# The last store of a fused attention and mixture kernel: four transfers cut by 32 partitions instead of by column block, a copy between the matmuls, another buffer for one scaled copy

## The chip, the core and the metric

The kernel runs on one core of one Trainium2 chip. A core has a matrix engine (TensorE; in the profile PE for its matmuls and PEld for its weight loads), a vector engine (VectorE, DVE), a scalar engine (ScalarE, ACT), a general engine (GpSimd, POOL) and a sync engine (SP) that only issues transfers; ACT and POOL issue transfers too. Transfers run on 16 DMA engines. Matmul results go to PSUM, whose banks hold 512 float32 per partition; everything else is in SBUF, 128 partitions wide.

The metric is device time in microseconds, the median of several executions. One execution was also profiled; its rows give a start and a duration for each instruction, counted from the start of its span.

## The reference, cut to what matters

```python
# attention: batch 4, heads 4, seq 1088, head_dim 32, r = 8
a = einsum('rd,bhsd->bhsr', S1, x);  b = einsum('rd,bhsd->bhsr', S2, x)
phi(x) = outer product of a and b, 64 features per row
kv = phi(k)^T v;  z = sum over s of phi(k)
attn = (phi(q) kv) / (phi(q) z + 1e-6)
x = attn, heads joined: 4352 rows of 128

# mixture: E = 4 experts, F = 1024 hidden
p = domain_probs / (sum(domain_probs) + 1e-9)
out = sum over e of p[:, e] * (relu(x @ w1[e]) @ w2[e])        # 4352 x 128, float32
```

## The kernel before, in words

The 4352 tokens are worked in ten chunks of 128, 448, seven times 480, and 416 columns. Tokens lie along the free dimension and the 128 features on the partitions; token t of a batch sits at row 34·(t mod 32) + t div 32 of that batch in DRAM, so that a block of 32 tokens has its rows 34 apart. For each chunk and each of the four experts the kernel makes eight blocks of 128 hidden rows (`first`: three matmuls a block, L1141, L1142, L1193) and multiplies them by the second weight matrix (`passed`: L1274). Matmuls of higher precision are made of several passes on split operands ("a", "b", "d"), which is why one expert has two PSUM accumulators, `o0` and `o1`. Which product is issued at which step is a list written by hand (`DEAL`, `DEAL_END` and others, worked off by `behind`); the schedule is manual, so each engine runs its instructions in the order in which the code emits them. The framework adds the semaphores, from the tiles that the instructions read and write.

When an expert is done, its `o0` is copied out by ACT with a scale of 1 + R12 (L1277) into the tile `ev`, `o1` is added, and the sum is multiplied by the gate and added to `total`. For most experts this is `close` and `gather`, partly on POOL (L1361, L1368, L1370). Where `gather` takes `o1` through ACT, the copy lies in a tile `rest` (L1358). Both `ev` and `rest` have one buffer.

The last expert of the last chunk (`at_end`: 416 tokens) goes another way, since nothing follows that could hide its end. `finish` does the three steps on DVE in two column halves, 256 and 160 (L1285, L1286, L1287), and leaves the sum with features on the partitions in `last_sum`. Two of the eight hidden blocks are multiplied with the tokens on the output's partitions (`by_token`, L1301): four column blocks `c` of 128, 128, 128 and 32 tokens in one PSUM bank `y`. Behind the second of them, four products of `last_sum` with an identity matrix (L1308, two matmuls each) turn the sum around and add it into the same bank. Then the bank is copied to `rows` in SBUF: ACT takes the first two column blocks (L1313), DVE the third and the fourth (L1314, L1315; the fourth has 32 partitions). Four transfers, one for each column block, send `rows` to `out` (L1318): SP block 0, ACT block 2, SP block 1, ACT block 3. In DRAM the access pattern of a transfer of 128 tokens begins with a dimension of 4, then 32 rows that lie 34 rows apart, then 128 contiguous floats; in SBUF it has 128 partitions of 128 floats.

The framework's closing instructions carry line L1534: SP waits there for every transfer, and then the engines meet.

Of the kernel before, what the change touches and what calls it, by code (L numbers as in the profile page):

```python
# [9 lines left out]
F32 = mybir.dt.float32  # L10
# [8 lines left out]
def _ap(t, p0: int, np_: int, off: int, free):  # L19

    p = list(t.ap)[0]
    return bass.AP(t.tensor, t.offset + p0 * p[0] + off, [[p[0], np_]] + [list(d) for d in free])
# [3 lines left out]
def kernel(  # L26
# [24 lines left out]
    nc = tc.nc  # L51

    P = 128
    HP = 64
    B, H, S, D = q.shape
    E, DM, F = w1.shape
    R = 8
    R2 = 2 * R
    G = S // 32
# [6 lines left out]
    CW = 480  # L66
# [48 lines left out]
    mpool = ctx.enter_context(tc.tile_pool(name="moe", bufs=2))  # L115
# [5 lines left out]
    def psum(pool, tag):  # L121
        return pool.tile([P, 512], F32, tag=tag, name=tag)
# [72 lines left out]
    def last_of(m, e, o):  # L195
        deal = deal_of(m, e)
        return max((p for p in deal if p[0] in ("ab" if o == 0 else "d" if at_end(m, e) else "dx")), key=lambda p: (deal[p], list(deal).index(p)))
# [4 lines left out]
    def second_weight(e, b):  # L202

        at = split_at(b)
        return w2_of[e, 0 if in_three(b) else 1][:, DM * at : DM * (at + 1)]
# [170 lines left out]
    def parts(m):  # L376

        c, end, at = START[m], START[m] + CHUNKS[m], 0
        while c < end:
            n = min(end, (c // S + 1) * S) - c  # L380
            yield c // S, c % S, n, at
            c, at = c + n, at + n
# [690 lines left out]
    def at_end(m, e):  # L1073
        return (m, e) == (NC - 1, E - 1)

    def block_of(m, e, k):
        return (THREE + tuple(OTHER))[k] if at_end(m, e) else k
# [180 lines left out]
    begun_o, evs = set(), {}  # L1258

    def passed(m, e, what, k, hd):  # L1260

        n, o = CHUNKS[m], 0 if what in "ab" else 1
        if what == "x" and at_end(m, e):
            return by_token(m, e, k, hd)
        if (m, e) not in acc:
            acc[m, e] = [None, None]
        if acc[m, e][o] is None:
            acc[m, e][o] = psum(ps_o, f"o{o}")
        first_one = (m, e, o) not in begun_o
        begun_o.add((m, e, o))  # L1270
        last = last_of(m, e, o) == what + str(k)
        b = block_of(m, e, k)
        w, h = (second_weight(e, b), hd) if what == "x" else (w2_parts[e][b]["abd".index(what)], hd["abd".index(what)])
        nc.tensor.matmul(acc[m, e][o][:, 0:n], w, h, start=first_one, stop=last)  # L1274
        if last and o == 0:
            evs[m, e] = mpool.tile([P, CW], F32, tag="ev", bufs=1, name="ev")
            nc.scalar.activation(evs[m, e][:, 0:n], acc[m, e][0][:, 0:n], ACTF.Copy, scale=1.0 + R12)  # L1277
        if last and o == 1:
            finish(m, e) if at_end(m, e) else close(m, e)

    def finish(m, e):

        n, o1, ev, g = CHUNKS[m], acc.pop((m, e))[1], evs.pop((m, e)), gate.pop((m, e))
        for x in (slice(0, 2 * P), slice(2 * P, n)):
            nc.vector.tensor_tensor(out=ev[:, x], in0=ev[:, x], in1=o1[:, x], op=ALU.add)  # L1285
            nc.vector.tensor_tensor(out=ev[:, x], in0=ev[:, x], in1=g[:, x], op=ALU.mult)  # L1286
            nc.vector.tensor_tensor(out=ev[:, x], in0=ev[:, x], in1=total[m][:, x], op=ALU.add)  # L1287
        last_sum[0] = ev
# [3 lines left out]
    def by_token(m, e, k, hd):  # L1292

        n = CHUNKS[m]
        if last_rows[0] is None:
            last_rows[0] = psum(ps_h, "h")
            last_rows.append(lpool.tile([P, 4 * P], F32, tag="kn", name="rows"))
        y, rows = last_rows
        cols = [(c, min(P, n - c)) for c in range(0, n, P)]
        for c, w in cols:  # L1300
            nc.tensor.matmul(  # L1301
                y[0:w, c : c + P], hd[:, c : c + w], second_weight(e, block_of(m, e, k)),
                start=(k == N3 and c == 0), stop=False, skip_group_check=True,
            )
        if k < FB - 1:
            return
        for c, w in cols:
            nc.tensor.matmul(  # L1308
                y[0:w, c : c + P], last_sum[0][:, c : c + w], eye[0][:, :],
                start=False, stop=True, skip_group_check=True,  # L1310
            )
        ((b, at, _, _),) = parts(m)
        nc.scalar.copy(rows[:, 0 : 2 * P], y[:, 0 : 2 * P])  # L1313
        nc.vector.tensor_copy(rows[:, 2 * P : 3 * P], y[:, 2 * P : 3 * P])  # L1314
        nc.vector.tensor_copy(rows[0 : n - 3 * P, 3 * P :], y[0 : n - 3 * P, 3 * P :])  # L1315
        for queue, c in ((nc.sync, 0), (nc.scalar, 2), (nc.sync, 1), (nc.scalar, 3)):
            c, w = cols[c]
            queue.dma_start(  # L1318
                bass.AP(out.tensor, out.offset + (b * S + (at + c) // 32) * DM, [[DM, w // 32], [G * DM, 32], [1, DM]]),
                rows[0:w, c : c + P],  # L1320
            )

    eye = [None]
# [91 lines left out]
    def close(m, e):  # L1415

        nonlocal ending
        ended = gather(m, e)
        next(ended)
        ending = chain(ending, ended)  # L1420
        closed[0] = m, e
# [5 lines left out]
    def behind(at):  # L1427

        was = closed[0]
        while due and due[0][0] <= at:  # L1430
            _, _, _, i, j, what = due.pop(0)
            m, kq = steps[i]
            e, f = divmod(kq, NP)
            if what:
                passed(m, e, what, 2 * f + j, hid[i][j])
                continue
            second(i, j)
            if i == NQ - 1:
                unit_project(0)
                unit_rows(0)  # L1440
            if f == NP - 1 and j == 1:
                close(m, e)
        return closed[0] != was
# [16 lines left out]
    for i in range(len(steps) + LA):  # L1460
# [4 lines left out]
        if i < len(steps):  # L1465
            m, kq = steps[i]
# [72 lines left out]
```

## Time and profile before

| what | value |
|---|---|
| median of 3 runs | 447.35 us (447.32 to 447.63) |
| the profiled execution: its own time | 447.11 us |
| its span, first to last instruction | 445.1 us |
| granted TensorE clock, mean | 0.997 |
| PE busy | 437.4 us, 98% |
| DVE busy | 386.5 us, 87% |
| ACT busy | 345.4 us, 78% |
| POOL busy | 166.7 us, 37% |
| last matmul of the program (L1308) ends | 438.94 us |
| last copy to `rows` (L1315) ends | 439.86 us |

A row of the timeline gives the start in the span, the duration, the engine and line, output <- inputs, the partitions and elements, and in brackets how long the engine had been idle before it and what it waited for. Rows that run together are merged ("x8"), and a merged row's second number is the stretch from its first start to its last end. "SPq" and "ACTq" are the queues of SP and ACT when they issue transfers: the duration is that of issuing, and the data moves afterwards. A table of stretches gives, for each, its length, the granted clock, the mean busy share of the 16 DMA engines and the GB/s they moved. "To landing" is the time from the start of a transfer's issue to its completion.

### The profile page before, as it was taken

Reading aid. Unit: us, or ns where it says so; the run is one execution under the profiler, and the core shown is the slowest. Engines: PE = TensorE matmul, PEld = TensorE weight load, DVE = VectorE, ACT = ScalarE, POOL = GpSimd, SP = SyncE. Lnnn points to the kernel's source line nnn. Section 1 sums busy time; section 2 is a strip of 40 time slices with the busy share of each in tenths; the row PEclk is TensorE's granted clock in tenths of the full one; section 3 lists DMA queues with packets and bytes.
Section 4 is the critical chain, followed back from the end, with each engine's and each line's share of the span. In section 5 each row is a group of like instructions: output and inputs, shape, how many; then the busy total and the mean of one; then the engine's idle time right before and its main releaser. Section 6 shows DMA issues by size and latency. Waiting matters only on the chain.

```text
span 445.1 us, 8123 instructions
## 1 busy us (share of the span) xinstructions
PE 437.4 (98%) x2770; PEld 359.6 (81%) x2770; DVE 386.5 (87%) x616; ACT 345.4 (78%) x721; POOL 166.7 (37%) x243
## 2 busy tenths in 40 slices
PE   9999999999999999999999999999999999999994
PEld 6887678888887887778887888787888888889992
DVE  5998979978999789989997898889988998899893
ACT  4478898848888688868884888687888888888881
POOL 6358523212142023213351354133335463555451
PEclk9999999999999999999999999999999999999998
DMA  7945375224602430235114511260420012002100
GB/s 224 307 114 170 86 174 112 73 56 122 149 24 45 123 90 24 74 83 143 24 28 74 143 19 41 50 159 21 71 50 21 18 46 45 23 13 43 26 20 21
DMA packets 45525, 35.02 MB, mean 79 GB/s; under 512 B 21708, under 2 KB 40268, under 8 KB 45484
## 3 DMA queue, kind: packets, MB, share of 16 engines
q1 hardware_dynamic: 43960, 33.30, 30.0%
q0 software_dynamic: 1184, 1.05, 1.0%
q8 instruction: 22, 0.36, 0.3%
q10 hardware_dynamic: 340, 0.15, 0.2%
q14 instruction: 19, 0.16, 0.1%
HBM read 29.27 MB, written 5.21 MB: 77 GB/s over the span
## 4 chain that ended last, share of the span: by engine, by line
PE 92%; DMA 3%; DVE 1%; SPq 1%; ACT 1%; issue 1%; POOL 0%; DVEq 0%; ACTq 0%
PE o L1274 40%; PE h L1141 14%; PE h L1142 14%; PE h L1193 14%; PE h L272 6%; PE o L1253 3%; DMA w_sb<-in_moe_w_dram 2%; PE h L459 1%; PE o L272 1%; DMA dp<-in_moe_domain_probs_dram 1%; PE h L1301 1%; DVE hb L1169 0%; ACT h L1143 0%; SPq L178 0%; DMA s_raw<-in_S_dram 0%
## 5 line engine op out<-in xcount | busy, mean ns | idle before, releaser
L1143 ACT ACTIVATE h<-h 128x480 f32<-128x480 f32 (+2 forms) x288 | 158.9, 552 | 63.8 <-PE h L1142 56.5
L1169 DVE SCALAR_TENSOR_TENSOR hb<-h,ha 128x480 fp32r<-128x480 f32 (+2 forms) x225 | 140.5, 639 | 28.2 <-ACT ha L1197 25.8
L1172 DVE SCALAR_TENSOR_TENSOR hd<-ha,hb 128x960 fp32r<-128x960 f32 (+4 forms) x120 | 137.9, 1149 | 11.6 <-DVE hb L1169 0.5
L1141 PE MATMUL h<-xa,wa 128*128 128x480 f32 (+2 forms) x288 | 129.5, 450 | 0.0
L1197 ACT ACTIVATE ha<-h 128x480 fp32r<-128x480 f32 (+2 forms) x225 | 126.3, 561 | 0.1
L1193 PE MATMUL h<-xd,wd 128*128 128x480 f32 (+2 forms) x288 | 108.7, 377 | 0.1
L1142 PE MATMUL h<-xb,wb 128*128 128x480 f32 (+2 forms) x288 | 108.0, 375 | 0.0
L1368 POOL TENSOR_TENSOR ev<-ev,gate 128x256 f32<-128x256 f32 (+3 forms) x52 | 46.8, 900 | 146.1 <-DVE ev L1355 138.4
L1274 PE MATMUL o<-ha,vab 128*128 128x480 f32 (+2 forms) x204 | 76.7, 377 | 0.0
L1141 PEld LDWEIGHTS h<-xa,wa 128*128 128x128 f32 x288 | 54.2, 188 | 18.0 <-issue 11.4
L1142 PEld LDWEIGHTS h<-xb,wb 128*128 128x128 f32 x288 | 54.2, 188 | 17.5 <-issue 11.7
L1274 PE MATMUL o<-hd,vd 128*128 128x480 f32 (+2 forms) x204 | 63.7, 379 | 0.2 <-DVE hd L1172 0.2
L1193 PEld LDWEIGHTS h<-xd,wd 128*128 128x128 f32 x288 | 54.0, 188 | 8.9 <-ACT h L1143 0.8
L1370 POOL TENSOR_TENSOR total<-total,ev 128x256 f32<-128x256 f32 (+3 forms) x52 | 55.7, 1072 | 4.1
L1274 PE MATMUL o<-hb,vb 128*128 128x480 f32 (+2 forms) x136 | 51.2, 376 | 0.0
L1274 PE MATMUL o<-hid,w_sb 128*128 128x480 f32 (+2 forms) x90 | 43.2, 561 | 0.0
L1274 PEld LDWEIGHTS o<-hd,vd 128*128 128x128 f32 x204 | 37.8, 188 | 6.3 <-issue 0.8
L1274 PEld LDWEIGHTS o<-ha,vab 128*128 128x128 f32 x204 | 38.3, 188 | 5.1
L1361 POOL TENSOR_TENSOR ev<-ev,rest 128x256 f32<-128x256 f32 (+2 forms) x24 | 16.9, 726 | 63.3 <-ACT rest L1358 63.3
L1207 ACT ACTIVATE hid<-h 128x480 f32<-128x480 f32 (+2 forms) x62 | 34.7, 560 | 1.5 <-PE h L1193 1.4
L1368 POOL TENSOR_TENSOR total<-ev,gate 128x256 f32<-128x256 f32 (+3 forms) x18 | 15.8, 898 | 38.4 <-issue 23.0
L1274 PEld LDWEIGHTS o<-hb,vb 128*128 128x128 f32 x136 | 25.5, 188 | 4.0 <-DVE hb L1169 0.4
(166 smaller groups left out, 466.8 us busy)
## 6 DMA issues: line engine op xcount, KB each, us to landing
gate<-gates SPq DMA_DIRECT2D x16, 240.0 KB, 3.4
kn<-in_k_dram SPq DMA_DIRECT2D x4, 544.0 KB
vn<-in_v_dram SPq DMA_DIRECT2D x16, 128.0 KB, 5.9
qp<-qd SPq DMA_DIRECT2D x8, 256.0 KB
qp<-qd SPq DMA_DIRECT2D x6, 288.0 KB, 4.7
qb<-qd SPq DMA_DIRECT2D x6, 288.0 KB
qn<-in_q_dram SPq DMA_DIRECT2D x3, 544.0 KB
w_sb<-in_moe_w_dram SPq DMA_DIRECT2D x3, 512.0 KB
```

The costliest lines, as they stand in the source:

```text
L272: nc.tensor.matmul(out(s), weights(s), moving(s), **flags)
L1141: nc.tensor.matmul(g, wa[:, e, w], xa, start=True, stop=False)
L1142: nc.tensor.matmul(g, wb[:, e, w], xb, start=False, stop=True)
L1143: nc.scalar.activation(g, g, ACTF.Copy, scale=1.0 + R12)
L1169: nc.vector.scalar_tensor_tensor(out=hb, in0=g, scalar=0.0, in1=high, op0=ALU.max, op1=ALU.subtract)
L1172: nc.vector.scalar_tensor_tensor(out=d2, in0=a2.bitcast(F32), scalar=R12, in1=b2.bitcast(F32), op0=ALU.mult, op1=ALU.subtract)
L1193: nc.tensor.matmul(g, w, x, start=False, stop=True, skip_group_check=True)
L1197: nc.scalar.activation(ha, g, ACTF.Relu, scale=NEAR)
L1207: nc.scalar.activation(hid[i][j], g, ACTF.Relu)
L1274: nc.tensor.matmul(acc[m, e][o][:, 0:n], w, h, start=first_one, stop=last)
L1368: nc.gpsimd.tensor_tensor(out=to[:, x], in0=ev[:, x], in1=g[:, x], op=ALU.mult)
L1370: nc.gpsimd.tensor_tensor(out=total[m][:, x], in0=total[m][:, x], in1=ev[:, x], op=ALU.add)
```

## The change

Three things, all at the last expert of the last chunk:

- the scaled copy of `o0` (L1277) goes to a tile with the tag `rest` instead of `ev`; `finish` works on that tile;
- in `by_token` the ACT copy of column blocks 0 and 1 is emitted behind the identity product of block 1, the DVE copy of block 2 behind that of block 2, and the DVE copy of block 3 behind that of block 3, where all copies stood behind all four products;
- the four transfers are cut by partitions: transfer `g` takes partitions 32g to 32g + 31 of all column blocks that have them (four for g = 0, three for the others). Its access pattern begins, on both sides, with a dimension of 32. SP sends g = 0 and 2, ACT sends g = 1 and 3. The 416 pieces of 512 bytes that are sent, and their places in DRAM, are the same.

```diff
         if last and o == 0:
-            evs[m, e] = mpool.tile([P, CW], F32, tag="ev", bufs=1, name="ev")
+            tag = "rest" if at_end(m, e) else "ev"
+            evs[m, e] = mpool.tile([P, CW], F32, tag=tag, bufs=1, name=tag)
             nc.scalar.activation(evs[m, e][:, 0:n], acc[m, e][0][:, 0:n], ACTF.Copy, scale=1.0 + R12)
...
         if k < FB - 1:
             return
-        for c, w in cols:
+        ((b, at, _, _),) = parts(m)
+        for i, (c, w) in enumerate(cols):
             nc.tensor.matmul(
                 y[0:w, c : c + P], last_sum[0][:, c : c + w], eye[0][:, :],
                 start=False, stop=True, skip_group_check=True,
             )
-        ((b, at, _, _),) = parts(m)
-        nc.scalar.copy(rows[:, 0 : 2 * P], y[:, 0 : 2 * P])
-        nc.vector.tensor_copy(rows[:, 2 * P : 3 * P], y[:, 2 * P : 3 * P])
-        nc.vector.tensor_copy(rows[0 : n - 3 * P, 3 * P :], y[0 : n - 3 * P, 3 * P :])
-        for queue, c in ((nc.sync, 0), (nc.scalar, 2), (nc.sync, 1), (nc.scalar, 3)):
-            c, w = cols[c]
-            queue.dma_start(
-                bass.AP(out.tensor, out.offset + (b * S + (at + c) // 32) * DM, [[DM, w // 32], [G * DM, 32], [1, DM]]),
-                rows[0:w, c : c + P],
+            if i == 1:
+                nc.scalar.copy(rows[:, 0 : 2 * P], y[:, 0 : 2 * P])
+            elif i > 1:
+                nc.vector.tensor_copy(rows[0:w, c : c + P], y[0:w, c : c + P])
+        for g in range(4):
+            t = len([w for _, w in cols if w > 32 * g])
+            (nc.scalar if g % 2 else nc.sync).dma_start(
+                bass.AP(out.tensor, out.offset + (b * S + at // 32 + g) * DM, [[G * DM, 32], [4 * DM, t], [1, DM]]),
+                _ap(rows, 32 * g, 32, 0, [[P, t], [1, DM]]),
             )
```

## The prediction, made before the result was known

> **What bounds the kernel now.** I read the page first: PE is busy 98% of the span, so up to the last matmul only PE's time counts. The change touches nothing before 434 us. What it touches lies in the last 11 us, and there PE is done at 438.94 while the span runs to 445.1: more than 6 us of copying, sending and closing. So I read the timeline of that end next.
>
> ```profile
> 434.23 0.34 PE L1274 MATMUL o<-hb,vb 128*128 128x416 f32 x1
> ...
> 434.77 0.65 PE L1274 MATMUL o<-hd,vd 128*128 128x416 f32 x2 [0.19 <-DVE hd L1172]
> ...
> 435.13 0.52 ACT L1277 ACTIVATE ev<-o 128x416 f32<-128x416 f32 x1 [0.57 <-POOL total L1370]
> ...
> 435.69 0.42 DVE L1285 TENSOR_TENSOR ev<-ev,o 128x256 f32<-128x256 f32 x1 [0.47 <-ACT ev L1277]
> ...
> 437.65 0.32 DVE L1287 TENSOR_TENSOR ev<-ev,total 128x160 f32<-128x160 f32 x1
> ...
> 437.67 1.27 PE L1308 MATMUL h<-eye,ev 128*128 128x128 f32 x8
> 438.98 0.37 ACT L1313 COPY rows<-h 128x256 f32<-128x256 f32 x1 [3.33 <-PE h L1308]
> 439.38 1.25 SPq L1318 DMA_DIRECT2D out_dram<-rows  x2
> 439.39 0.29 DVE L1314 COPY rows<-h 128x128 f32<-128x128 f32 x1 [1.42 <-ACT rows L1313]
> 439.59 0.27 DVE L1315 COPY rows<-h 32x128 f32<-32x128 f32 x1
> ```
>
> See two things. The DVE copy L1314 reads and writes other columns than the ACT copy L1313, yet it waited for it: the program orders accesses of two engines to the one PSUM bank, even two reads. That order is not one of `rows`, since SP's first transfer left at 439.38 without waiting for the DVE copies into the same tile. And the copies take 0.9 us in all (438.98 to 439.86); the other 5 us are transfers and closing. So I asked for those: the last issue on ACT's queue and its landing, and the share of the 16 DMA engines by stretch, here and where the kernel stores 128 pieces of 512 bytes elsewhere (L722).
>
> ```profile
> 440.46 0.46 ACTq L1318 DMA_DIRECT2D out_dram<-rows  x1
> ```
> ```profile
> out_dram<-rows ACTq DMA_DIRECT2D x1, 16.0 KB, 3.5
> ```
> ```profile
> 440.90:441.50 0.60, 1.00 0.28 79
> 441.50:441.90 0.40, 1.00 0.24 46
> 441.90:442.40 0.50, 1.00 0.34 88
> 442.40:442.70 0.30, 1.00 0.43 101
> 442.70:443.30 0.60, 0.51 0.30 90
> 443.30:443.50 0.20, 0.50 0.16 44
> ```
> ```profile
> 198.60:199.20 0.60, 1.00 0.72 168
> ```
>
> The last transfer, of only 16 KB, was issued at 440.46 and landed 3.5 us later, at 443.96; the rest of the span, 1.1 us, is closing. From 440.9 to 443.3 the data moved without a break, but at about 0.3 of the engines' time, some four to five of 16. At 198.6 to 199.2 stores of the same piece or a little larger kept 0.72 busy. The end is bound by transfers that use a quarter of the DMA engines.
>
> **The change part by part.**
>
> *The other buffer.* L1277 waited 0.57 us for POOL, which held `ev`. The tile `rest` was last read by POOL at 421.4 (L1361), so L1277 can start when its bank is done: 434.23 + 0.34 = 434.57, about 434.6 instead of 435.13. L1285 then waits for `o1`, whose last matmul ends at 434.77 + 0.65 = 435.42: 435.46 instead of 435.69, 0.23 us sooner. None of it counts: the first half of the sum was ready at 437.03 (L1287: 436.60 + 0.43) for a product that PE reached at 437.67, and the second half at 437.97 for block 2, which PE reached at 438.11. What covers it is PE's own row of 16 matmuls L1301 ahead. The ACT order is unchanged, and nothing else on SP or POOL is passed. Zero; without that cover the gain would be 0.23 at most.
>
> *The copies between the products.* The first two column blocks are in PSUM at 438.39 (the timeline cut at that place gives 437.89 + 0.50). If bank order holds for a matmul behind a read as it does for a read behind a read, each later step waits for the one before. Hand-overs from the rows: PE to ACT 0.04 (438.94 to 438.98), ACT to PE 0.05 (L1143 ends 428.96, the weight load of L1193 starts 429.01), DVE to PE 0.05 (L1172 ends 434.72, L1274 loads at 434.77). One block of two matmuls from a standing start takes 0.49 (437.67 to 438.16), the block of 32 takes 0.41 (438.54 to 438.94). Sum: ACT copy 438.39 + 0.04 + 0.37 = 438.80; block 2 on PE + 0.05 + 0.49 = 439.34; DVE copy + 0.04 + 0.29 = 439.67; block 3 + 0.05 + 0.41 = 440.13; DVE copy + 0.04 + 0.27 = 440.44. Before, the last copy ended at 439.86: 0.58 later. Queued behind the waits on PE is only the rest of this chain; behind those on DVE nothing; on ACT the transfers. The nearest row for PE's restart is L1301 after its wait, and it shows nothing longer. If the matmuls did not wait, the copies would end at about 439.30 (ACT 438.80, DVE + 0.03 + 0.29, and the last one 0.20 + 0.27 - 0.29 behind), 0.56 sooner.
>
> The Trainium skill, in "PSUM — Partial Sum Buffer", section "PSUM bank collisions raise a hardware error", says that no two of the three engines may touch the same bank and quadrant at once and that programs must guard PSUM by bank, not by address. By that rule the sum is the one with the waits, 440.44; without it, 439.30. The wait of 1.42 on L1314 agrees, between two reads; no row of before shows a matmul behind such a read.
>
> *The transfers.* Removed: three of 64 KB and one of 16; added: one of 64 and three of 48, the same 416 pieces. SP's pair begins when the last copy is done (g = 0 needs block 3): 440.44 + 0.03 = 440.47 instead of 439.38. ACT's pair needs blocks 0 to 2 only: 439.67 + 0.03 = 439.70, as before (439.71), its second issue 0.75 behind as before, 440.45. The second SP issue comes 0.47 behind the first by L722 (four issues in 1.85, one 0.45) or 0.67 by L1318 (439.38 to 440.05). I take 0.5, since the form of L722 is nearer. From issue to landing I have these rows, all stores out of 32 partitions, of L722 and then L1336:
>
> ```profile
> DMA to landing us min/median/max: 1.7/1.7/1.7
> ```
> ```profile
> DMA to landing us min/median/max: 1.6/1.9/2.5
> ```
>
> L722 is the same form: 32 partitions, four pieces of 512 bytes from each, to DRAM. I take 1.8, with 1.6 and 2.5 as ends. SP's second lands at 440.47 + 0.5 + 1.8 = 442.77; ACT's second at 440.45 + 1.8 = 442.25. The last landing moves from 443.96 to 442.77: 1.2 us sooner. The closing 1.1 us stays.
>
> Why 1.8 and not 3.5: the old patterns began with a dimension of 4, and a quarter of the engines was busy; L722's begin with 32. The Trainium skill states it so in "DMA: Bandwidth & Descriptors", section "Why a DMA increments its semaphore by 16 and not by 1": a transfer runs on the largest number of engines up to 16 that divides the slowest dimension of both patterns, here 4 before and 16 after. The share of 0.28 agrees.
>
> *Sum.* SP's first issue is 1.09 later (0.58 from the copies; 0.51 because it left before the DVE copies and now waits for them), and from there to the last landing 4.58 become 2.30: together -1.2 us on the span. The profiled execution took 447.11 (span 445.1 and 2.0 around it), which becomes 445.9; it was 0.24 below the median of the runs shown. Against the median, 447.35 - 1.2 = 446.15.
>
> **The rivals.**
>
> *PE is not held.* If the products of blocks 2 and 3 run on while ACT copies, SP starts at 439.33 and its second transfer lands at 439.33 + 0.5 + 1.8 = 441.63: -2.3, 445.0. For it: different columns. Against it: L1314's wait.
>
> *Transfers at the slow end.* Issue 0.67 apart and 2.5 to landing (16 engines that all read the same 32 partitions and write while ACT's pair does): 440.47 + 0.67 + 2.5 = 443.64, -0.3, 447.0, no difference. For it: L1336's worst. Against: L722 had four in a row at 1.7.
>
> *The other side: the transfers stay slow, and the chain of copies is all that is felt.* From the first issue to the last landing the four took 443.96 - 439.38 = 4.58 us. If that stays, counted from SP's new first issue at 440.47, the last lands at 445.05: +1.1, 448.45. It is slower by over 0.2% (0.9 us, about what a measurement of this kernel can tell from no change) once the four take over 4.39. Counted from ACT's first issue, 439.70, it would be +0.3 and no difference. For it: at 442.4 to 442.7, when the old transfer with 32 rows ran beside the others, the share rose only to 0.43. Against it: 0.72 in L722. The Trainium skill speaks for it too, in the table "Rules for kernel authors" of "DMA: Bandwidth & Descriptors": do not bother to cut a transfer into disjoint groups of partitions, as they share the same engines. The trace's 0.28 says that here they did not.
>
> *The pattern does not do what it says*, sending as before: that is the case above.
>
> **How the numbers follow.** The forecast has 0.73, with 445.8 to 446.6 as its own range (landing 1.6 to 2.0, issue 0.47 to 0.67). PE not held: 0.08, at 445.0. Slow end: 0.11, at 446.6 to 447.3. The other side: 0.08, of which 0.06 above 448.2. The range 445.5 to 447.0 leaves out the first and the last rival and a part of the third, under 0.2. Faster by over 0.2% means below 446.45: 0.08, and 0.69 of the forecast's 0.73: 0.77. Slower, above 448.25: 0.06. The same: 0.17.
>
> **What would show it.** L1277 starts near 434.6 with no wait for POOL, and L1308 still begins at 437.67. L1308's later blocks wait, PEld for ACT and then for DVE, about 0.4 each, and L1315's successor ends near 440.4. SP issues at 440.5 and 441.0, with 0.45 each instead of 0.6. The share of the DMA engines passes 0.5, and the four transfers land within 1.6 to 2.0 of their issue. Wrong would be: no PE wait (then 445.0), or a DMA share of 0.3 once more, or closing work that does not move with the last landing.

## The result and the profile after

The changed kernel takes 446.03 us (median of 8 runs, 445.53 to 447.24), the kernel before beside it 447.36 (8 runs, 447.32 to 447.74). The ratio is 0.997, with a 95% interval of 0.9959 to 0.9981: faster by 1.33 us, 0.3%. Forecast were 446.15 and a range of 445.5 to 447.0.

The profiled execution is the longest of the eight: 447.24 us, span 445.4. It must be read with that in mind, and the experiments below say what was different in it. Its end first, in the timeline; in the changed kernel the scaled copy is L1278, the identity products L1310, the copies L1315 and L1317, the transfers L1320.

```profile
434.64 0.52 ACT L1278 ACTIVATE rest<-o 128x416 f32<-128x416 f32 x1
...
437.69 0.71 PE L1310 MATMUL h<-eye,rest 128*128 128x128 f32 x4
438.44 0.37 ACT L1315 COPY rows<-h 128x256 f32<-128x256 f32 x1 [3.29 <-PE h L1310]
438.87 0.30 PEld L1310 LDWEIGHTS h<-eye,rest 128*128 128x128 f32 x2 [0.65 <-ACT rows L1315]
...
439.39 0.29 DVE L1317 COPY rows<-h 128x128 f32<-128x128 f32 x1 [1.41 <-PE h L1310]
439.72 0.84 ACTq L1320 DMA_DIRECT2D out_dram<-rows  x2
439.74 0.14 PEld L1310 LDWEIGHTS h<-eye,rest 128*32 128x32 f32 x2 [0.57 <-DVE rows L1317]
...
440.18 0.28 DVE L1317 COPY rows<-h 32x128 f32<-32x128 f32 x1 [0.50 <-PE h L1310]
440.52 0.83 SPq L1320 DMA_DIRECT2D out_dram<-rows  x2
```

L1278 no longer waits for POOL, and nothing at the end moves for it: the products still begin at 437.69. They now run in three pieces. PE waits for the ACT copy and then for the DVE copy, and the last copy ends at 440.46 instead of 439.86. SP's two issues come 1.14 later than before and take 0.83 together instead of 1.25.

The busy share of the DMA engines by stretch (length, granted clock, share, GB/s) shows both the gain and what was odd in this execution:

```profile
440.60:441.20 0.60, 0.89 0.44 111
441.20:441.60 0.40, 0.50 0.86 192
441.60:442.00 0.40, 0.50 0.48 119
442.00:442.50 0.50, 0.50 0.22 52
442.50:443.00 0.50, 0.50 0.02 2
443.00:443.50 0.50, 0.50 0.08 9
443.50:444.00 0.50, 0.50 0.03 9
```

The table counts a piece whole in the stretch in which it starts. The 0.86 so holds 0.26 of an instruction transfer (1.67 us on one engine, below); the stores alone come to 0.60, about twice the 0.28 of before, and they are nearly through by 442.5. Then, from 443, a little more than one engine in 16 (0.08) still moves data. In the stretch from 441.2 to 443.0 the list of queues and issues has these lines:

```profile
q8 instruction: 1, 0.02, 5.8%
...
out_dram<-rows SPq DMA_DIRECT2D x1, 48.0 KB, 3.5
```

One transfer of instructions, 16 KB, took 5.8% of 16 engines over 1.8 us: 1.67 us of one engine. The last store took 3.5 us to land, as long as before, although fifteen of its sixteen shares had landed by 442.6 in the trace. The closing work of 1.0 us follows.

### The profile page after: what moved, and what is told of

It is laid out like the page before. It is cut to its first block, busy times and chain, and to the rows that moved or that the text cites. A ratio compares the mean times of both kernels' runs of the same rounds, so it can differ in the third digit from the quotient of the medians.

```text
span 445.4 us, 8125 instructions
## 1 busy us (share of the span) xinstructions
PE 437.1 (98%) x2770; PEld 359.4 (81%) x2770; DVE 386.7 (87%) x616; ACT 345.4 (78%) x721; POOL 166.3 (37%) x243
## 4 chain that ended last, share of the span: by engine, by line
PE 95%; DVE 2%; DMA 1%; ACT 1%; issue 1%; SPq 0%; ACTq 0%; DVEq 0%
PE o L1274 40%; PE h L1141 14%; PE h L1142 14%; PE h L1193 14%; PE h L272 7%; PE o L1253 3%; PE o L272 2%; PE h L459 1%; DMA kn<-in_k_dram 1%; PE h L1302 1%; DVE hb L1169 0%; ACT h L1143 0%; PE h L1310 0%; DVE hd L1172 0%; DVE qp L587 0%
```

## The experiments

Times are medians, ratios those to the kernel before on the same chip. The kernel before was at 447.19 (23 runs) beside the first four of these kernels, and at 447.44 (9 runs) beside the old cut, the second bank, the second run of the transfers alone and the first of the moved instructions. Beside the two single runs at the end it took 447.51 (one run). Single traces begin the identity products anywhere from 437.4 to 438.1, so places at the end are compared from that start.

**The other buffer alone.**

```diff
-            evs[m, e] = mpool.tile([P, CW], F32, tag="ev", bufs=1, name="ev")
+            tag = "rest" if at_end(m, e) else "ev"
+            evs[m, e] = mpool.tile([P, CW], F32, tag=tag, bufs=1, name=tag)
```

> Only the other buffer: the scaled copy of o0 goes to the tile rest, copies and transfers as before. Theory (PE's own row of matmuls covers it): L1277 starts near 434.6 with no wait for POOL, L1308 still begins at 437.67, time 447.35 within 0.15. Rival (the sum of the last expert gates the identity products): the 0.23 us that DVE gains reach the end, 447.1.

447.34 us, ratio 1.0002 (0.9993 to 1.0011). The span is 445.1 as before. The part is worth nothing here: the products begin at 437.69, as good as the 437.67 of before, behind PE's own matmuls. The 0.23 us that DVE was to gain did not arrive either. Its first step began 0.14 sooner (435.55 instead of 435.69), but the last step (L1288 here) now has a semaphore instruction of its own ahead of it in each half, the gap before it is 0.11 instead of 0.04, and the second half ended at 437.99 instead of 437.97.

**The transfers alone.** Copies behind all four products, as before; `rows` is sent by partitions.

```diff
-        for queue, c in ((nc.sync, 0), (nc.scalar, 2), (nc.sync, 1), (nc.scalar, 3)):
...
+        for g in range(4):
+            t = len([w for _, w in cols if w > 32 * g])
+            (nc.scalar if g % 2 else nc.sync).dma_start(
...
```

> Only the four transfers cut by 32 partitions; copies behind all four products and tile ev as before. Theory (the transfers run on 16 DMA engines instead of 4, and the interleaved copies of the changed kernel cost 0.58): last copy ends at 439.86, SP issues at 439.9 and 440.3, all land by 442.0 to 442.4, 1.5 to 2.0 sooner than before: 445.4 to 445.9, below the changed kernel's 446.03. Rival (the copies between the products are part of the gain): no faster than 446.0.

445.2 us, ratio 0.9959 (0.9947 to 0.9972): faster than the whole change, which took 445.77 in the same group (below), and below the 445.4 to 445.9 expected. Its timeline, and its share of the DMA engines:

```profile
437.89 1.27 PE L1308 MATMUL h<-eye,ev 128*128 128x128 f32 x8
439.20 0.37 ACT L1313 COPY rows<-h 128x256 f32<-128x256 f32 x1 [3.33 <-PE h L1308]
439.61 0.29 DVE L1314 COPY rows<-h 128x128 f32<-128x128 f32 x1 [1.41 <-ACT rows L1313]
439.81 0.27 DVE L1315 COPY rows<-h 32x128 f32<-32x128 f32 x1
439.93 0.84 ACTq L1318 DMA_DIRECT2D out_dram<-rows  x2
440.16 0.81 SPq L1318 DMA_DIRECT2D out_dram<-rows  x2
```
```profile
441.20:441.60 0.40, 1.00 0.90 219
441.60:442.00 0.40, 0.50 0.53 141
442.00:442.50 0.50, 0.50 0.00 0
```

SP issues 2.27 after the products' start; in the changed kernel it is 2.83 (440.52 - 437.69). That is the 0.56 that the interleaved copies cost, and the medians differ by 0.57. The transfers alone are worth 2.0.

**The copies alone.** The products and copies as in the changed kernel, the old transfers.

```diff
+            if i == 1:
+                nc.scalar.copy(rows[:, 0 : 2 * P], y[:, 0 : 2 * P])
+            elif i > 1:
+                nc.vector.tensor_copy(rows[0:w, c : c + P], y[0:w, c : c + P])
```

> Only the copies between the products; transfers by column block and tile ev as before. Two effects oppose each other. Bank order makes the last copy end at 440.44, 0.58 later; but the first transfer needs only the first copy and leaves at 438.83 instead of 439.38. If the four slow transfers, one behind the other on four engines, set the end, they start 0.55 sooner and the time is 446.8 to 447.0. If the last copy sets the end (block 3 is sent 0.6 later), it is 447.9.

446.75 us, ratio 0.9987 (0.9978 to 0.9995): a little faster, as the first branch has it.

```profile
438.11 0.71 PE L1309 MATMUL h<-eye,ev 128*128 128x128 f32 x4
438.85 0.37 ACT L1314 COPY rows<-h 128x256 f32<-128x256 f32 x1 [2.77 <-PE h L1309]
439.25 1.26 SPq L1319 DMA_DIRECT2D out_dram<-rows  x2
...
440.60 0.28 DVE L1316 COPY rows<-h 32x128 f32<-32x128 f32 x1 [0.50 <-PE h L1309]
```

SP starts 1.14 after the products' start instead of 1.71, while the last copy is late by the same 0.6 as in the changed kernel. With transfers that queue on four engines, the early first send is worth more than the late last copy costs. So the sooner copy helps the old transfers and hurts the new ones, all of which need block 2, and g = 0 block 3.

**The changed kernel again**, for a second trace.

> The changed kernel itself once more, for a second trace. In its first trace 15 of 16 shares of each of the last three transfers had landed by 442.6, and the last share came at 444.0 to 444.4; an instruction transfer of 16 KB ran on one engine from 441.2 to 442.9. Theory (the last instruction fetch of PE, about 1 us behind PE's last instruction, holds one DMA engine in the middle of the transfers): the fetch is there again near 441.2, and one share in 16 is late again, by more or less as the fetch takes long; median 446.0, span of the trace 443.6 to 445.4. Rival (a single disturbance of one execution): no late share in this trace, span 443.8.

445.77 us, ratio 0.9969 (0.9958 to 0.998). The trace shows an instruction transfer from 441.5, a share of 0.08 of the engines at 443.0 to 443.5 and a span of 445.4 again, in an execution of 447.28; the other six of the kernel's executions took 445.57 to 446.66. In the sixteen executions of this kernel on record the span was 445.4 in the two traced ones and at most 444.6 in the others.

**The old cut on 16 engines.** The kernel before, with the two outer dimensions of the DRAM pattern exchanged. It keeps the bytes and the pieces, but not the order of the rows: within a block they go to other places of `out` than the reference has them.

```diff
-                bass.AP(out.tensor, out.offset + (b * S + (at + c) // 32) * DM, [[DM, w // 32], [G * DM, 32], [1, DM]]),
+                bass.AP(out.tensor, out.offset + (b * S + (at + c) // 32) * DM, [[G * DM, 32], [DM, w // 32], [1, DM]]),
```

> The kernel before, its transfers still cut by column block, with the two outer dimensions of the DRAM pattern exchanged, so that it begins with 32 and not with 4. The rows of a block so land in another order in their places of out: the order is changed, the bytes, pieces and issues are the same. Theory (the size of the first dimension sets the number of engines): issues at 439.4, 439.7, 439.8 and 440.1, landing 1.7 after each, the last at 441.9, 2.0 sooner than before: 445.2 to 445.4. Rival (the cut into groups of 32 partitions is what makes them faster): 447.2, share of the DMA engines 0.3.

445.48 us, ratio 0.996 (0.9946 to 0.9974). The share of the engines, and the issues:

```profile
441.20:441.60 0.40, 1.00 0.63 186
441.60:442.00 0.40, 0.71 0.65 187
442.00:442.50 0.50, 0.50 0.00 0
```
```profile
L1318 SPq DMA_DIRECT2D out_dram<-rows x2: 594/602/611, 439.6 to 440.3; - x2
```

The share doubles and the data is through by 442.0 without any cut by partitions. The issues are longer than expected: they take 0.54 to 0.65 instead of about 0.4, the last starts at 440.71 instead of 440.1, and the time is a little above the 445.2 to 445.4 expected. Exchanging the two dimensions gives 1.96 us, of the 2.16 that the transfers alone gave beside it (below). How many engines worked can be counted as well. Beside the 416 pieces of 512 bytes the trace has small pieces, which belong to none of them; at the end of the kernel before and of this one:

```profile
DMA packets 446, 0.24 MB, mean 34 GB/s; under 512 B 28, under 2 KB 444, under 8 KB 444
DMA packets 482, 0.23 MB, mean 29 GB/s; under 512 B 64, under 2 KB 480, under 8 KB 480
```

With one small piece for each engine that a transfer uses, 64 is four transfers on 16 engines, and 28 is three on 4 and one, that of 16 KB, on 16. The updates of the transfers' semaphores in the trace agree: behind the data there are 4, 4, 4 and 16 before, and 16 for each transfer here and in the changed kernel. The exchange also puts four neighbouring rows behind one another; that is not what makes it fast, since the pieces of the changed kernel lie four rows apart and have 64 small pieces too. So the size of the first dimension is the cause.

**A second PSUM bank.** The changed kernel with column blocks 2 and 3 in a bank of their own, and the DVE copies behind the last product.

```diff
-            last_rows[0] = psum(ps_h, "h")
+            last_rows[0] = psum(ps_h, "h"), psum(ps_h, "h")
...
-                y[0:w, c : c + P], last_sum[0][:, c : c + w], eye[0][:, :],
+                y[c // 256][0:w, c % 256 : c % 256 + P], last_sum[0][:, c : c + w], eye[0][:, :],
...
+        for c, w in cols[2:]:
+            nc.vector.tensor_copy(rows[0:w, c : c + P], y[1][0:w, c % 256 : c % 256 + P])
```

> The changed kernel with column blocks 2 and 3 in a second PSUM bank, and the two DVE copies behind the last product; so no product has to wait for a copy. Theory (bank order alone holds PE, at 0.45 and 0.38 in the trace of the changed kernel): the eight identity matmuls run through again in 1.27, ACT copies beside them, the last copy ends about 0.78 behind the last product's start at 438.67, near 439.45, SP issues at 439.5 and 439.9, all lands by 441.6, 1.0 sooner than the undisturbed shares of the changed kernel (442.6): 445.0. Rival (PE waits for something else, or the copies on ACT and DVE hold each other back in spite of two banks): last copy at 440.4 as in the changed kernel, 446.0; or at 439.9 as before, 445.2.

445.18 us, ratio 0.9945 (0.9932 to 0.9957), the lowest of all.

```profile
437.70 1.27 PE L1310 MATMUL h<-eye,rest 128*128 128x128 f32 x8
438.45 0.37 ACT L1315 COPY rows<-h 128x256 f32<-128x256 f32 x1 [3.29 <-PE h L1310]
439.01 0.48 DVE L1317 COPY rows<-h 128x128 f32<-128x128 f32 x2 [1.02 <-PE h L1310]
439.38 0.84 ACTq L1320 DMA_DIRECT2D out_dram<-rows  x2
439.56 0.81 SPq L1320 DMA_DIRECT2D out_dram<-rows  x2
```

With two banks PE is not held, the ACT copy runs beside the products, and the last copy ends at 439.49. SP issues 1.86 after the products' start, 0.97 sooner than in the changed kernel. The wait of block 2 for the ACT copy is gone although that copy stands where it stood, so the shared bank caused it (the bank is also one tile, and which of the two the program orders by is not told apart here). The wait of block 3 is gone because the DVE copies stand behind it; that the bank caused that one too is argued.

**The transfers alone again**, beside the second bank.

> The new transfers alone once more, beside the second bank: 445.2 as in its first run. Theory: the second bank is faster than this by 0.2 to 0.4, since its copies end 0.4 sooner; rival: equal, if the landing of the last transfer no longer follows the copies.

445.28 us, ratio 0.9953 (0.9939 to 0.9966). SP issues 2.26 after the products' start, so the second bank sends 0.4 sooner, but the medians are only 0.1 apart and the runs overlap (444.75 to 445.31 against 444.84 to 446.01). Both beat the kernel before and the changed one; which of the two is faster is not settled. In the one trace of each, the time between the last landing and the end of the span is 1.4 us with the second bank (441.73 to 443.1) and 1.0 here (441.82 to 442.8). Of the difference, 0.3 lies between two of SP's closing instructions, 0.36 apart there and 0.05 here; why was not pursued.

**PE's instructions moved by two places.** The changed kernel with one warming matmul fewer at the start.

```diff
-    keep_warm(11)
+    keep_warm(10)
```

> The changed kernel with one warming matmul fewer at the start (10 instead of 11), so that PE's instructions stand two places further on and instruction transfers fall elsewhere; everything at the end is the same. Theory (the 16 KB instruction transfer makes the late share): if the trace has no such transfer between 440 and 444, all 16 shares land together and the span is 443.6; if it still has one near 441.3, one share is late again. Rival (the late share comes from the stores themselves): late share at 444.0 to 444.4 without an instruction transfer near it.

445.95 us, ratio 0.9962 (0.995 to 0.9975), like the changed kernel. The trace has no 16 KB instruction transfer at the end:

```profile
441.20:441.60 0.40, 0.60 0.47 119
441.60:442.00 0.40, 0.50 0.66 161
442.00:442.50 0.50, 0.50 0.42 104
442.50:443.00 0.50, 0.50 0.00 0
443.00:443.50 0.50, 0.50 0.00 0
```
```profile
out_dram<-rows SPq DMA_DIRECT2D x1, 48.0 KB, 1.7
```

All shares land together, the last store 1.7 after its issue, and the span is 443.8.

**Both once more, for their traces.**

> The changed kernel a third time, for its trace. Theory (the 16 KB instruction transfer stands at this place of the program and makes the late share whenever the engine it runs on has stores queued): the transfer near 441.3, one share of 16 late, span about 445.4. Rival (chance): no late share, span near 443.8.

> The changed kernel with one warming matmul fewer, a second time, for its trace. Theory: no 16 KB instruction transfer before the last landing, all 16 shares together, span about 443.8. Rival (chance): a late share now and then here too.

The shifted kernel gave 446.11 us in one run, with all shares together and a span of 444.0, as expected. The changed kernel gave 445.86 in one run, and there the expectation missed: no late share, span 443.9. The instruction transfer was there, but at 439.6. In the stretch from 439.6 to 440.6, ahead of every store, the queues show

```profile
q8 instruction: 1, 0.02, 5.9%
```

and it was over before the first store's data moved. So its place is not fixed by the program. What holds over all traces with stores on 16 engines: in the two where a 16 KB instruction transfer ran among them, one share in 16 was late by 1.6 us or more and the span was 445.4; in the seven where none did, none was late. The times in the two late traces say how. In the first the instruction transfer starts at 441.27 and takes 1.67 us, to 442.94. Around that end the share of the stores, and the pieces from 442.90 to 443.77, are

```profile
442.30:442.90 0.60, 0.50 0.00 0
442.90:443.00 0.10, 0.50 0.09 10
DMA packets 23, 0.01 MB, mean 12 GB/s; under 512 B 3, under 2 KB 23, under 8 KB 23
```

No store's piece starts between 442.30 and 442.90; the late ones start at 442.92, one behind the other. They are 20 pieces of 512 bytes and three small ones, one share in 16 of the last three transfers. In the second trace the instruction transfer ends at 443.03 and the late share, again 23 pieces, begins at 443.01. So in both it held one engine's share until it was done. It could not be placed at will, and what decides when it runs stays open.

## Why the prediction was right

*The other buffer* was put at zero with PE's 16 matmuls as its cover. Alone it gave a ratio of 1.0002. Right, though the gain that was to be covered, 0.23 us, was itself too large: 0.14 at DVE's first step and nothing at its last.

*The copies between the products* were the step with the least support, since no row showed a matmul behind a copy from the same bank. The chain came out nearly as summed: block 2 began 0.06 behind the ACT copy (0.05 taken), block 3 0.06 behind the DVE copy, and the last copy ended at 440.46 against a forecast of 440.44. The kernel with the second bank has neither wait, the first of them for the bank, the second because its copies stand elsewhere. The rule of the Trainium skill, in "PSUM — Partial Sum Buffer", section "PSUM bank collisions raise a hardware error", to guard PSUM by bank and not by address, is what the program did, at a price of 0.56.

*The transfers* were expected on 16 engines instead of 4, from the share of 0.28. Exchanging the two dimensions alone took 1.96 us off, which agrees with how the Trainium skill, in "DMA: Bandwidth & Descriptors", section "Why a DMA increments its semaphore by 16 and not by 1", counts the engines. The 16 KB transfer of before is counted there with those on four engines, but its pattern starts with 32 rows and it ran on 16 engines: twelve of its sixteen semaphore updates came by 443.14, the last four from 443.52 to 443.96. Only the other three were on four. Two terms were too large. SP's second issue came 0.39 behind the first (440.52 to 440.91), not 0.5: both rows that I took it from were of issues of 0.45 and more, and the first here took 0.34. And from issue to landing it was 1.7 in the undisturbed traces of this kernel, not 1.8, as L722 had said. Together 0.2, and 0.3 with the closing work, which took 1.0 instead of 1.1; the two measurements, at -1.3 and -1.4, lie 0.1 to 0.2 below the forecast of -1.2, to within their scatter. That 1.7 held was in part luck: it is one landing, that of the first of L722's 28 issues, and the profile gives none for the others, so no row shows "four in a row at 1.7".

*The rivals.* PE was held, so the first fell. Its end was nearly reached by another kernel, the one with two banks, at 445.18 where 445.0 had been worked out. The slow end, landing 2.5 us after issue or later, did not set the median, but in two traced executions the last landing took 3.2 and 3.5 us, for a reason that was not on the list: one engine in 16 behind an instruction transfer. The other side fell with the share of 0.66 in the shifted kernel's trace. The advice of the Trainium skill, in the table "Rules for kernel authors" of "DMA: Bandwidth & Descriptors", not to cut transfers by partitions is borne out in this way: the cut itself brought little (445.28 against 445.48 for the old cut with the dimensions exchanged), the first dimension nearly everything.

*What would show it* was seen: L1278 at 434.64 with no wait, products at 437.69, two waits of PE (its matmuls stood 0.46 and 0.38, its weight loads 0.65 and 0.57), issues of 0.34 to 0.44, a share above 0.5. Not foreseen was that "land within 1.6 to 2.0" would fail in the very trace that was taken.

## What to carry to other kernels

Where a kernel ends on its stores, look at the mean share of the DMA engines over that stretch: a quarter can mean, as it did here, that the transfers use four engines of sixteen, and exchanging two dimensions of an access pattern may be worth more than any reordering of the work before it. A copy put between matmuls of the same PSUM bank did not overlap them here but cut them apart; give the later part its own bank, or leave the copies behind. And test the parts of a change alone: here one part won 2.0 us, one lost 0.56 of it, and one did nothing.

## What the runs showed of the hardware that I had not expected

- Issuing a store from 32 partitions took 0.34 to 0.44 us on SP, from 128 partitions 0.58 to 0.62, with 4 engines and with 16 alike (the kernel before and the old cut on 16 engines). The number of engines is not what makes the issue long. Nor is it the partitions alone: ACT's transfer of 16 KB, from 32 partitions, took 0.46 before and 0.54 in the old cut on 16 engines.
- An instruction transfer of 16 KB held one DMA engine for up to 1.7 us. With stores spread over all engines, each transfer has a share on that engine, and two of the nine traces with such stores, both of the changed kernel, ended some 1.5 us later than its third trace. That wider transfers are more exposed to it than those on four engines is argued, not shown.
- The same early copy is a gain of 0.4 us with the old transfers (0.9987) and a loss of 0.56 with the new: what the copy order is worth depends on which transfer waits for which block.
